# When token chunks enter a wavelet-MLP kernel: two at a time at both ends of the entry, or one per visit throughout

## The chip, the cores and the metric

The kernel runs on one core of one Trainium2 chip. The metric is device microseconds of the whole program. A core has TensorE (PE, matmuls, with PEld for the loading of their stationary operand), VectorE (DVE), ScalarE (ACT), GpSimd (POOL) and SyncE (SP). DMAs are issued from the queues of POOL, SP and ACT and are carried out by the core's 16 DMA engines.

## The reference, cut to what matters

`x` is (8, 4224, 192): batch, tokens, channels. A causal convolution of 7 taps per head runs first, and its result goes into a phase mixer whose large part is a product over all tokens.

```python
# first part: softmax over the 7 taps of each of 8 heads, then
out[b, s, h*24+g] = sum_k w[h, k] * x_pad[b, s + k, h*24+g]      # 6 zero rows ahead
# second part, on x = out
theta = x @ w_theta                       # 192 x 192
zr, zi = x * cos(theta), x * sin(theta)
y = w_tok_r @ zr + w_tok_i @ zi           # 4224 x 4224 over tokens, for each batch
u = x + y
result = u + max(u @ w_ch, 0)
```

## The kernel before

**Tiles.** Batch and channel together are 1536 columns (`N`), in two halves of 768 (`HN`) and four of 384 (`PC`, one PSUM bank in float32). The tokens that are summed over are cut into 33 *chunks* (`NCH`) of 128 tokens. A chunk is four quarters of 32 tokens that lie 33x32 tokens apart (`tokens`). The tokens of the result are cut into 17 *units* (`UNITS`): sixteen pairs of 128-token tiles, and one single tile (unit 16).

**A chunk** is made so. A *window* (class `Window`, L253) is three quarters with the six tokens ahead of each, loaded from `x` by three DMAs on POOL's queue into one of three `xw` tiles (L267). It is convolved by eight matmuls against banded weights (L304) and copied from PSUM into an `xz` tile (L183 on DVE or L185 on ACT). So three chunks take four windows; a chunk's four quarters lie in two or three of them. When a window has been convolved, the next free one is loaded. A chunk (class `Chunk`, L342) is then kept in HBM (`xs`, SP's queue, L355), transposed (L475 on PE for the first eleven chunks, by DMA later), multiplied by `w_theta` (L490), clamped (L378, DVE), and sine and cosine are taken (L406, ACT). The products with x (L415, DVE) and five differences (L427, DVE) leave seven z tiles in one of 11 slots (`SLOTS`).

**A visit** (class `Visit`, L642) is one unit of result rows multiplied with all chunks that are resident in the slots at that time: 14 products of 384 columns for each chunk and visit of a pair (a Strassen-Winograd form of the two-by-two block product), 8 for the single unit (L702, PE). The visit's weights (class `Weights`, L504) are eight DMAs on POOL's queue, four quarters each of `moe_w_tok_r` and `moe_w_tok_i`, cast to bfloat16 into two `st` tiles, one for each matrix (L523). DVE transposes them from there into `w` tiles (L545) and forms four sums or differences (L559). The partial sums of a unit are four `d` tiles in float32. They are loaded from HBM (SP's queue, L664, `d<-part`) when the unit has been visited before, added to from PSUM (L726, twelve times in a visit), and stored again (L741, `part<-d`). Two more evictions of a visit are copies between PSUM banks (L185). In one visit of each unit the convolved x is added to the sums as well (`xr` loads, L671, and additions on POOL, L674). In a unit's last visit the result is finished instead of stored: cast (L836, ACT), transposed, multiplied by `w_ch` (L490), added (L855, DVE) and written out (L862, SP's queue).

**Which chunks are in which visit** is a matter of one tuple, `FIRST`: the visit in which each of the first eleven chunks enters. A chunk stays for 17 visits, so that it has met every unit, and the chunk that takes over its slot enters 17 visits after it:

```python
FIRST = (0, 0, 1, 2, 3, 4, 5, 6, 7, 8, 8)
...
enter = list(FIRST)
for c in range(SLOTS, NCH):
    enter.append(enter[c - SLOTS] + UNITS)
...
for v in range(enter[-1] + UNITS):
    here = [c for c in range(NCH) if enter[c] <= v < enter[c] + UNITS]
    visits.append((ORDER[v % UNITS], here[0], here[-1] + 1))
...
settled = enter[-1]
extra = [v for v in range(len(visits)) if visits[v][2] - visits[v][1] <= SMALL][-EXTRA:]
extra = [v for v in extra if v > settled]
...
    sequence.insert(settled + 2 + 3 * k, v)
```

With it there are 59 visits: 0 to 7 hold 2 to 9 chunks, 8 to 50 hold 11, and 51 to 58 hold 9 down to 2. Chunks enter in visits 0 to 8, 17 to 25 and 34 to 42. The last visits of at most three chunks (`EXTRA` of them at most, here 57 and 58) are taken out of the end and put in between the visits after the last entry: the order there is 42, 43, 58, 44, 45, 57, 46 and so on to 56. `residual_at` (L152) says in which visit a unit gets the convolved x.

**The order of the work.** Each piece above is a `Step` with an engine and an estimated duration. A planner (class `Schedule`, L1005) plays the steps through twice, from due times that come from when the products are wanted, and the second time writes each engine's instructions out in the order that it found. On each engine, and in each issuing queue, the order is then fixed: a step that waits holds up all that stands behind it. The planner picks the PSUM banks of the short matmuls and, for some copies, the engine.

Of the kernel before, what the change touches and what calls it, by code (L numbers as in the profile page):

```python
# [16 lines left out]
def kernel(  # L17
# [39 lines left out]
    NG = 2  # L57
    UNITS = (NT + 1) // 2
    SLOTS = 11
    FIRST = (0, 0, 1, 2, 3, 4, 5, 6, 7, 8, 8)  # L60
    CLAMP = 1.5
    EXTRA = 3
    BY_PE = 4
# [47 lines left out]

    enter = list(FIRST)
    for c in range(SLOTS, NCH):
# [1031 lines left out]
```

## Time and profile before

| | us |
|---|---|
| time, median of 3 runs | 1582.66 |
| lowest and highest run | 1582.4, 1584.01 |
| the profiled execution, its own time | 1582.66 |
| its span, first to last instruction | 1580.9 |

The profile shows one execution. A row of instructions gives engine, operation, output from input, the count, and the mean time of one. A stretch gives for each engine how long it was busy, then the granted TensorE clock as a share of full speed, the DMA share and GB/s. The DMA share is the summed time of packets over that of 16 engines. Packets that overlap each count, so it can pass 1.

The granted clock over the span is 0.956. Four kinds of transfer make up most of the traffic: partial sums (384 KB each, 164 stores, 150 loads of the tile `d` and 14 of the tile `late`, landing after 6.0 to 6.9 us in the median), weights (472 loads, 176 KB each with 11 chunks, 9.8 us), x (132 loads, 114 KB, 14.8 us) and the results (66 stores of 384 KB, 5.0 to 5.5 us).

### The profile page before, as it was taken

Reading aid. Unit: us, or ns where it says so; the run is one execution under the profiler, and the core shown is the slowest. Engines: PE = TensorE matmul, PEld = TensorE weight load, DVE = VectorE, ACT = ScalarE, POOL = GpSimd, SP = SyncE. Lnnn points to the kernel's source line nnn. Section 1 sums busy time; section 2 is a strip of 40 time slices with the busy share of each in tenths; the row PEclk is TensorE's granted clock in tenths of the full one; section 3 lists DMA queues with packets and bytes.
Section 4 is the critical chain, followed back from the end, with each engine's and each line's share of the span. In section 5 each row is a group of like instructions: output and inputs, shape, how many; then the busy total and the mean of one; then the engine's idle time right before and its main releaser. Section 6 shows DMA issues by size and latency. Waiting matters only on the chain.

```text
span 1580.9 us, 24396 instructions
## 1 busy us (share of the span) xinstructions
PE 1434.5 (91%) x9318; PEld 898.2 (57%) x9318; DVE 1076.6 (68%) x1781; ACT 430.7 (27%) x761; POOL 616.7 (39%) x766
## 2 busy tenths in 40 slices
PE   4678899999989989798999996997979999979998
PEld 2345566666655556464666654564646666646665
DVE  5667775435576678566756775865769887666787
ACT  3566461112433124220000321232332212111132
POOL 7645451212543455422312543643534344531220
PEclk6899999999999999898999998998999999999999
DMA  8999998547999999998978999999997999999994
GB/s 60 126 152 167 172 161 153 108 104 134 177 202 225 182 193 216 211 179 170 229 181 178 199 192 166 207 199 196 166 220 179 238 255 236 224 173 196 209 231 151
DMA packets 615269, 289.20 MB, mean 183 GB/s; under 512 B 438800, under 2 KB 565776, under 8 KB 615152
## 3 DMA queue, kind: packets, MB, share of 16 engines
q0 software_dynamic: 451392, 101.19, 61.9%
q1 hardware_dynamic: 123760, 176.62, 40.9%
q10 hardware_dynamic: 40000, 9.84, 4.8%
q8 instruction: 73, 1.20, 0.3%
q14 instruction: 44, 0.36, 0.1%
HBM read 251.60 MB, written 103.42 MB: 225 GB/s over the span
## 4 chain that ended last, share of the span: by engine, by line
PE 50%; DMA 37%; POOL 5%; issue 4%; DVE 3%; SPq 1%; DVEq 0%; ACT 0%; POOLq 0%; ACTq 0%
PE bank L702 46%; DMA xw<-in_x_dram 18%; DMA st<-in_moe_w_tok_i_dram 5%; DMA st<-in_moe_w_tok_r_dram 5%; PE bank L490 3%; DMA xr<-xs 3%; POOL xw L267 2%; DMA uT<-xz 2%; DMA d<-part 1%; DMA part<-d 1%; DMA out_dram<-d 1%; DVE w L545 1%; POOL st L523 1%; POOL d L674 1%; DVE d L726 1%
## 5 line engine op out<-in xcount | busy, mean ns | idle before, releaser
L702 PEld LDWEIGHTS <-w 128*128 128x128 bf16 x7586 | 744.2, 99 | 538.2 <-issue 76.7
L702 PE MATMUL bank<-t,w 128*128 128x384 bf16 x3204 | 567.9, 328 | 11.0 <-DVE d L726 10.1
L545 DVE STREAM_TRANSPOSE w<-st 128x640 bf16<-128x640 bf16 (+4 forms) x412 | 342.9, 856 | 257.1 <-DMA st<-in_moe_w_tok_r_dram 103.2
L702 PE MATMUL bank<-r,w 128*128 128x384 bf16 x2158 | 404.5, 333 | 32.2 <-DVE d L726 16.9
L702 PE MATMUL bank<-i,w 128*128 128x384 bf16 x2224 | 398.8, 330 | 22.1 <-DVE d L726 20.0
L726 DVE TENSOR_TENSOR d<-bank,d 128x384 f32<-128x384 f32 x516 | 275.8, 543 | 155.1 <-PE bank L702 129.9
L523 POOL DMA_DIRECT2D st<-in_moe_w_tok_r_dram x236 | 136.3, 585 | 388.1 <-DVE w L545 333.1
L523 POOL DMA_DIRECT2D st<-in_moe_w_tok_i_dram x236 | 135.4, 579 | 265.5 <-DMA xw<-in_x_dram 128.5
L267 POOL DMA_DIRECT2D xw<-in_x_dram x132 | 189.3, 1440 | 98.9 <-PE bank L304 45.5
L559 DVE TENSOR_TENSOR w<-w 128x1408 bf16<-128x1408 bf16 (+8 forms) x216 | 182.4, 844 | 2.3
L185 ACT ACTIVATE xz<-bank 32x384 bf16<-32x384 f32 (+2 forms) x299 | 139.9, 482 | 147.6 <-issue 84.0
L674 POOL TENSOR_TENSOR d<-d,xr 128x768 f32<-128x768 f32 x60 | 100.6, 1678 | 115.8 <-DMA xr<-xs 58.3
L185 ACT ACTIVATE bank<-bank 128x384 f32<-128x384 f32 x109 | 51.1, 474 | 240.3 <-PE bank L702 232.2
L406 ACT ACTIVATE r<-ang,half_pi 128x768 bf16<-128x768 f32 x44 | 41.0, 932 | 276.0 <-DVE ang L378 275.8
L185 ACT ACTIVATE d<-bank 128x384 f32<-128x384 f32 x127 | 60.8, 490 | 159.9 <-PE bank L702 159.4
L490 PE MATMUL bank<-wth,uT 128*128 128x192 bf16 x528 | 67.4, 269 | 34.6 <-DVE ang L378 20.2
L378 DVE TENSOR_SCALAR ang<-bank 128x384 f32<-128x384 f32 x132 | 70.0, 549 | 34.8 <-PE bank L490 33.9
L490 PEld LDWEIGHTS <-uT 128*128 128x128 bf16 x632 | 60.4, 106 | 56.6 <-issue 27.3
L304 PE MATMUL bank<-xw,bands 114*128 114x192 bf16 x352 | 54.3, 255 | 27.8 <-DMA xw<-in_x_dram 8.5
L836 ACT ACTIVATE ubT<-d 128x768 bf16<-128x768 f32 x42 | 35.4, 842 | 160.3 <-DVE d L726 146.5
L304 PEld LDWEIGHTS <-bands 114*128 114x128 bf16 x352 | 34.7, 101 | 47.7 <-issue 21.1
L855 DVE SCALAR_TENSOR_TENSOR d<-bank,d 128x384 f32<-128x384 f32 x104 | 53.8, 547 | 10.8 <-PE bank L490 9.8
(76 smaller groups left out, 563.8 us busy)
## 6 DMA issues: line engine op xcount, KB each, us to landing
part<-d SPq DMA_DIRECT2D x164, 384.0 KB, 6.7
d<-part SPq DMA_DIRECT2D x150, 384.0 KB, 6.9
st<-in_moe_w_tok_r_dram POOLq DMA_DIRECT2D x160, 176.0 KB, 9.8
st<-in_moe_w_tok_i_dram POOLq DMA_DIRECT2D x160, 176.0 KB, 9.8
out_dram<-d SPq DMA_DIRECT2D x52, 384.0 KB, 5.5
xw<-in_x_dram POOLq DMA_DIRECT2D x131, 114.0 KB, 14.8
xs<-xz SPq DMA_DIRECT2D x132, 96.0 KB, 8.4
xr<-xs POOLq DMA_DIRECT2D x66, 192.0 KB, 8.4
```

What stands on the lines that cost most here:

```text
L185: act(nc.scalar.activation(out=o(), in_=i(*b), func=AT.Copy))
L267: pool(nc.gpsimd.dma_start(out=xw[self.k][lo : lo + n, :, :], in_=x[:, t0 : t0 + n, :].rearrange("b s d -> s b d"),))
L304: pe(nc.tensor.matmul(banks[b][:, hh * B * G : (hh + 1) * B * G], lhsT=bands[:, h, at : at + NQ, :].rearrange("p z m -> p (z m)"), rhs=xw[ ...
L378: "dve", 0.55, lambda b, k2=k2, g=g: dve(nc.vector.tensor_scalar(out=self.ang[g][:, k2 * 2 * D : (k2 + 1) * 2 * D], in0=banks[b][:, 0 : 2 ...
L490: pe(nc.tensor.matmul(banks[bk][:, b * D : (b + 1) * D], lhsT=tT[:, 3 * k + b + i, :], rhs=w[:, 2 * b + i, :], start=(i == 0), stop=(i == ...
L523: "pool", 0.58, lambda a=a, t0=t0, i=i, w=w: pool(nc.gpsimd.dma_start(out=st[i][a * Q : (a + 1) * Q, 0:nb, 0 : n * Q], in_=w[r0 : r0 + nb ...
L545: lambda c=c, ce=ce: dve(nc.vector.transpose(self.tile(name)[:, c:ce, :, :], st[i][:, at : at + NQ, c * Q : ce * Q].rearrange("p bt (c j) ...
L559: s = Step("dve", 0.15 + 0.069 * n, lambda: dve(nc.vector.tensor_tensor(out=flat(self.tile(name)), in0=flat(self.tile(p)), in1=flat(self.t ...
L674: a = Step("pool", 1.75, lambda: pool(nc.gpsimd.tensor_tensor(out=tile_(), in0=tile_(), in1=xrt[k], op=ALU.add)), [r, s])
L702: pe(nc.tensor.matmul(banks[bank][:, 0:PC], lhsT=self.w.block(a, c), rhs=chunks[c].operand(b, g), start=(start and c == self.lo), stop=(c ...
L726: dve(nc.vector.tensor_tensor(out=o, in0=y, in1=o, op=ALU.add))
L855: dve(nc.vector.scalar_tensor_tensor(out=dk, in0=banks[b][:, 0:PC], scalar=0.0, in1=dk, op0=ALU.max, op1=ALU.add,))
```

## The change

One line: the first chunk enters in visit 0, the next in visit 1, and so on to chunk 10 in visit 10.

```diff
@@ -57,7 +57,7 @@
     NG = 2
     UNITS = (NT + 1) // 2
     SLOTS = 11
-    FIRST = (0, 0, 1, 2, 3, 4, 5, 6, 7, 8, 8)
+    FIRST = (0, 1, 2, 3, 4, 5, 6, 7, 8, 9, 10)
     CLAMP = 1.5
     EXTRA = 3
     BY_PE = 4
```

What follows from it in the lists: 61 visits; 0 to 9 hold 1 to 10 chunks, 10 to 50 hold 11, and 51 to 60 hold 10 down to 1. Chunks enter one in a visit, in visits 0 to 10, 17 to 27 and 34 to 44. The visits that are put in between the others are 60, 59 and 58, and the order at the end is 44, 45, 60, 46, 47, 59, 48, 49, 58, 50, 51 and so on to 57. The planner plays the steps through anew, so the order on every engine can differ everywhere.

## The prediction

> **What bounds the kernel now.** I read the head of the page first.
>
> ```profile
> span 1580.9 us, 24396 instructions
> PE 1434.5 (91%) x9318; PEld 898.2 (57%) x9318; DVE 1076.6 (68%) x1781; ACT 430.7 (27%) x761; POOL 616.7 (39%) x766
> ...
> PE   4678899999989989798999996997979999979998
> ...
> DMA  8999998547999999998978999999997999999994
> ```
>
> PE is the bound, with 146 us of idle in 1580.9. The DMA digits fall below 9 where PE stays at 9 (slices 7 to 10, 21 and 22). So the idle has to be looked for by stage. I counted the products of line 702 in order of time (14 per chunk and visit, 8 for unit 16) to find where each visit starts, and asked for the busy table of those stretches. Neighbouring visits interleave a little, so the limits are good to about 1 us.
>
> ```profile
> 54.60:79.20 24.60, 14.48 (x84) 8.54 (x84) 13.49 (x29) 12.83 (x26) 13.10 (x14) 0.81 1.14 144
> 218.70:246.30 27.60, 27.60 (x189) 17.65 (x188) 23.55 (x40) 12.63 (x22) 10.66 (x15) 1.00 1.35 162
> 411.10:443.40 32.30, 29.39 (x205) 18.88 (x203) 20.89 (x30) 15.07 (x28) 17.01 (x15) 1.00 1.34 197
> 530.60:570.90 40.30, 30.83 (x180) 18.86 (x179) 23.70 (x38) 7.61 (x14) 20.82 (x24) 0.87 1.29 207
> 570.90:597.90 27.00, 27.00 (x180) 17.03 (x179) 22.86 (x38) 8.05 (x14) 14.52 (x16) 1.00 1.28 192
> 729.50:754.50 25.00, 25.00 (x155) 15.05 (x154) 15.83 (x25) 0.95 (x2) 4.55 (x8) 1.00 0.87 199
> 1219.30:1282.40 63.10, 62.70 (x434) 40.80 (x432) 55.78 (x95) 12.50 (x18) 29.32 (x40) 1.00 1.12 238
> ```
>
> After the stretch come its length, then busy time of PE, PEld, DVE, ACT and POOL, granted clock, DMA share and GB/s. The rows are visits 1, 8, 16, 20, 21, 26, and 43+58+44. A full visit (11 chunks) in which no chunk enters takes 25.0 us at DMA share 0.87; one in which a chunk is prepared takes 27.0 us when it goes well, so a chunk's convolution and mix cost PE 2.0 us. While chunks enter, the DMA share is about 1.3, and some visits are far longer.
>
> The second entry (visits 16 to 25) took 32.3, 29.9, 29.1, 28.2, 40.3, 27.0, 27.7, 39.4, 29.4 and 35.1 us: 318.4, where 10x25.0 + 11x2.0 = 272 are needed, so 46 us are lost. The third (33 to 42) took 32.7, 27.7, 45.8, 27.0, 29.8, 42.1, 27.0, 29.6, 37.9 and 25.0: 324.6, 53 lost. The waits, over the whole span, tell what the lost time is (us in total, times, longest):
>
> ```profile
> PE bank L702 <- DVE d L726: 47.1, 16, 11.5
> ...
> PE bank L490 <- DVE ang L378: 20.2, 7, 6.7
> ...
> DVE w L545 <- DMA st<-in_moe_w_tok_r_dram: 103.2, 14, 19.2
> ...
> POOL st L523 <- DMA xw<-in_x_dram: 175.3, 65, 6.5
> ```
>
> Read upwards: POOL's queue holds weight loads back until x loads have landed; the weights come late; DVE stands in order at the transpose; the evictions queued behind it (L726, L378) come late, and PE has no bank. The long visits are 20, 23, 25 and 35, 38, 41. Windows hold three quarters and a chunk four, so every third chunk (12, 15, 18, 21, 24, 27, 30) needs two windows, and each convolved window releases three x loads. The long visits are those that take in chunks 15, 18, 21 and 24, 27, 30. They are bursts, tied to chunks.
>
> **The change part by part.** The chunk-visits stay 561, so products, conversions, x loads and mixes stay the same in number. From the lists of lines 112 to 128: 61 visits in place of 59; sizes 1 to 10 at the start, eleven from visit 10 to 50, then 10 down to 1. In all, two visits of 11 become two of 10 and two of 1. Chunks enter one per visit at 0 to 10, 17 to 27 and 34 to 44. The lists of residual visits come out the same, so 43 and 44, which have one, now lie inside the third entry.
>
> Two visits add: 16 weight loads (POOL, 585 ns each by the L523 rows: 9.4 us), eight loads and eight stores of 384 KB on SP's queue (units 11 and 7 get a fourth visit; their last visits, 59 and 60, go between 45 and 50), and 24 evictions of 543 ns (13.0 us of DVE). None of it is PE work. All of it lies beside PE unless a queue is late, so I price it by stage.
>
> *Start.* Visit k now needs chunk k, where visit k-1 needed it. So new visit k answers to old visit k-1, with one chunk-visit more done (14 matmuls, about 2.3 us) and one weight set more loaded: that of one chunk. POOL pays 8x0.58 = 4.6 us for it in the queue in which the x loads stand, and its loads must land: the nearest rows are those of two chunks (32.0 KB), 2.8 and 6.0 us median. 4.6 + 4 (between these) - 2.3 = +6, less what idle POOL hides (13.1 busy of 24.6 in visit 1): **+4**. Lower end -2 (all hidden, one chunk-visit gained); upper end: the second rival below. Chunk 10's later date gains nothing: visit 8, which takes chunks 9 and 10, already runs without PE idle.
>
> [...] No run here has shown a set of one chunk.
>
> *Second entry.* What goes is the double entry: visit 16 at 32.3 us against 25.0 + 2x2.0 = 29, and visit 25, which took two chunks and three windows. From the first 3 us come back; of the second's 8 over 27.0 only 1, since chunk 21 still has its burst. Against that chunk 12's burst moves from the relaxed visit 16 to visit 17, where loads are already dense: +2. Sum **-2**; ends -17 (two visits' worth of relief, first rival) and +4 (third rival).
>
> *Third entry.* Double entry gone: 32.7 against 29, -3. Residual visits 43 and 44 now meet x loads: four residual loads and four adds each, 4x(0.6+1.65) = 9 us of POOL per visit in front of weight loads; visit 42 had 25.0 us with no wait at all. A burst stall is 11 to 19 us here (37.9 to 45.8 less 27.0); I take less than half of one, +5. Sum **+2**; ends -17 and +26.
>
> The clock is a part of each stall: visit 20 lost 13.3 us, of which its waits are 9.4 (6.3 on L378 and 3.1 on L726); the rest goes with its clock of 0.87. The prices above are whole visit times and hold this already. [...]
>
> *Final part.* Visit 60 (one chunk) has its fixed work: 12 evictions x 0.543 = 6.5, eight output additions (L855, 0.547) = 4.4, small transposes and sums 3 (bounded by the rows of two chunks, 0.44 and 0.29 each): 14 us of DVE where PE works 14x0.161 + 32x0.08 = 5 (25.0 us for 154 products, and half of that for the 32 narrower output matmuls). The excess of 9 meets the slack of its neighbours: 63.1 - 55.8 = 7 in the last row of the table, for three visits. So 2 stay, and 2 more for the 16 transfers of 384 KB beside DMA share 1.12: **+4**. Ends 0 and +9.
>
> Sum: +4 - 2 + 2 + 4 = +8. The profiled execution took 1582.66 us, span 1580.9 and 1.8 around it, and is the median itself. 1582.66 + 8 = 1590.7.
>
> **The rivals.** *Relief (faster).* If the entries are bound by DMA throughput and not by bursts, spreading wins. Clean stretches move about 0.84 of a share (47.5% + 36.3% of the two big queues, 720 to 880 us) in 25 us, 21 units a visit; entries run at 1.30. A visit more in an entry then costs 21/1.30 = 16 us there and takes 25 us out of the clean stretch: -9 per entry for one visit, -17 for two. For it: every entry visit stands at 1.28 to 1.35. Against it: visits 21 and 22 run at 27.0 and 27.7 at that same share. It decides if a burst's stall shrinks below about 8 us. 4 + 4 - 9 - 9 = -10: 1572.7.
>
> *Start paced by weight sets.* Old visits 0 to 8 start at 27.3, 54.6, 79.2, 104.7, 123.4, 145.7, 171.8, 194.5 and 218.7 us, and sets are issued some 21 us apart, whatever their size. If each new visit still takes its old slot, visit 10 starts with 55 chunk-visits done instead of 66: 11x2.27 = 25 us instead of 4: 1612. Against it: the first set is small and visit 0 waits for no second chunk.
>
> *The dense rate holds throughout.* Visits 18 to 24 average 31.6 us and 35 to 41 average 34.2, with one chunk each. Eleven such visits and a clean one are 372.6 and 401 us, against 368.4 and 375 for the same twelve visits now: +4 and +26. With 4 and 4: 1620.7. Against it: three windows are loaded before each entry, and the third entry's last chunks release no loads.
>
> *No net effect.* Terms of single microseconds cancel; 1582.7.
>
> **How the numbers follow.** A measurement of this kernel tells about 0.2% (3.2 us) from no change. Forecast 0.38, relief 0.32, set-paced start 0.10, dense rate 0.08, no net effect 0.12. So faster 0.32, within 0.2% 0.12, slower 0.56. The forecast's own range, from its terms, is 1586 to 1604. To hold 8 in 10, it goes down to 1566, taking in relief but for its far end, and up to 1616, with the set-paced start and without the dense rate.
>
> **What would show it.** L523 with 488 issues, part<-d with 172. Visit 10 starting near 250 us with 55 chunk-visits done (start +4); near 271, the set-paced rival. Long visits at 21, 24, 27 and 36, 39, 42, each 35 us or more, and visit 16 near 27: bursts. If these fall under 33 us, relief was right. Visit 60's neighbours over 29 us would confirm the final term. I am wrong if PE's idle falls below 140 us.

## The result, and the profile after

| | before | after |
|---|---|---|
| median of four runs, us | 1583.34 | 1596.04 |
| lowest and highest | 1582.4, 1584.57 | 1591.87, 1616.18 |
| profiled execution, its span | 1580.9 | 1595.0 |

The changed kernel is slower, by under 1%: ratio 1.0071, 95% interval 1.0049 to 1.0093. The forecast was 1590.7 us, slower. A second comparison, told below, gave 1.0121 (1.0066 to 1.0177). Ratios here and below leave out single runs more than 1.5% above the fastest of their kernel: 1616.18 here, and seven of the ten runs of the pair-at-end kernel below.

The head of the page after:

```profile
span 1595.0 us, 24505 instructions
...
PE 1442.9 (90%) x9318; PEld 900.5 (56%) x9318; DVE 1085.3 (68%) x1823; ACT 429.5 (27%) x763; POOL 623.6 (39%) x782
...
PE   4668998999979969799899997798989999899998
...
DMA  8999998467999999999879999999999999999994
```

PE has the same 9318 matmuls. It idles 152 us (1595.0 - 1442.9) where it idled 146, and the other 8 us of the 14 stand as busy time (1442.9 against 1434.5), with the mean granted clock at 0.953 in place of 0.956. DVE's count grew by 42, POOL's by 16, the added weight loads. Visits can be found as before, by counting the products of line 702. The rows below are visits 1, 9, 16, 18, 21, 22, 24, 48 and 45+60+46; the columns are those shown of before (length, busy PE, PEld, DVE, ACT, POOL, clock, DMA share, GB/s):

```profile
45.90:68.40 22.50, 12.34 (x71) 6.64 (x72) 13.51 (x30) 11.19 (x20) 13.70 (x16) 0.75 1.13 140
223.00:255.30 32.30, 27.24 (x178) 17.22 (x176) 19.50 (x32) 12.54 (x23) 10.83 (x15) 0.95 1.12 148
394.70:422.60 27.90, 27.21 (x180) 16.96 (x178) 16.63 (x26) 12.09 (x22) 12.01 (x13) 1.00 1.17 149
452.70:489.30 36.60, 29.97 (x181) 18.16 (x179) 23.68 (x41) 7.61 (x14) 11.21 (x15) 0.91 1.33 203
544.10:588.50 44.40, 31.49 (x180) 18.93 (x178) 25.09 (x38) 7.61 (x14) 21.33 (x24) 0.85 1.27 181
588.50:615.50 27.00, 27.00 (x180) 17.05 (x178) 22.10 (x38) 8.05 (x14) 18.16 (x20) 1.00 1.10 222
643.60:684.70 41.10, 30.55 (x180) 18.75 (x178) 23.64 (x42) 7.61 (x14) 11.45 (x16) 0.88 1.30 199
1342.50:1379.80 37.30, 31.20 (x205) 19.71 (x203) 25.19 (x42) 5.71 (x8) 14.12 (x20) 0.95 1.21 228
1256.40:1321.70 65.30, 63.51 (x429) 40.58 (x427) 50.85 (x93) 12.78 (x18) 24.73 (x35) 0.97 0.99 210
```

The bursts are there, each one visit later: chunks 12, 15 and 18 enter in visits 18, 21 and 24, which take 36.6, 44.4 and 41.1 us. The two windows of such a chunk are convolved in the visit before; the long visit is the next one, where the late weights are missed. Visit 22, after such a burst, takes the full-speed 27.0. The doubled visit 16 is gone (27.9 in place of 32.3). New are visit 9 at 32.3 us and visit 48 at 37.3.

The waits of the whole span, after, with the chain that the prediction read (us in total, times, longest):

```profile
PE bank L702 <- DVE d L726: 40.2, 15, 10.0
PE bank L490 <- DVE ang L378: 35.2, 10, 6.7
...
PE bank L702 <- DVE w L545: 20.4, 5, 9.7
...
DVE w L545 <- DMA st<-in_moe_w_tok_r_dram: 115.0, 20, 16.0
...
POOL st L523 <- DMA xw<-in_x_dram: 193.1, 75, 8.0
```

POOL's queue holds weight loads back behind x loads for 193 us instead of 175, and DVE waits longer for weights.

To compare times at equal work, I take the moments when 66, 264 and 429 chunk-visits are done. Before, these are the starts of visits 10, 28 and 43; after, of 11, 29 and 44. Each kernel has two traces, the second from the runs told below. All in us:

| stretch | before, two traces | after, two traces | difference of the means | forecast |
|---|---|---|---|---|
| start, to 66 | 271.4, 267.7 | 280.3, 278.3 | +9.7 | +4 |
| second entry, to 264 | 508.1, 515.5 | 515.6, 523.7 | +7.9 | -2 |
| third entry, to 429 | 439.8, 437.6 | 435.5, 430.1 | -5.9 | +2 |
| final part, to the end | 361.6, 353.9 | 363.6, 366.7 | +7.4 | +4 |

Two executions of one kernel differ by up to 8 us in a stretch, so of these differences only that of the start stands well clear of the scatter. The first traces alone give +8.9, +7.5, -4.3 and +2.0, which is the 14.1 us between the spans.

### The profile page after: what moved, and what is told of

The parts are those of the page before. It is cut to its first block, busy times and chain, and to the rows that moved or that the text cites. A ratio compares the mean times of both kernels' runs of the same rounds, so it can differ in the third digit from the quotient of the medians.

```text
span 1595.0 us, 24505 instructions
## 1 busy us (share of the span) xinstructions
PE 1442.9 (90%) x9318; PEld 900.5 (56%) x9318; DVE 1085.3 (68%) x1823; ACT 429.5 (27%) x763; POOL 623.6 (39%) x782
## 3 DMA queue, kind: packets, MB, share of 16 engines
q0 software_dynamic: 455744, 101.19, 60.6%
## 4 chain that ended last, share of the span: by engine, by line
DMA 29%; PE 27%; issue 7%; POOL 6%; DVE 4%; SPq 1%; ACTq 0%; ACT 0%; DVEq 0%; POOLq 0%
PE bank L702 24%; DMA st<-in_moe_w_tok_r_dram 10%; DMA st<-in_moe_w_tok_i_dram 7%; DMA xw<-in_x_dram 6%; POOL xw L267 3%; PE bank L490 2%; POOL d L674 2%; DVE w L545 2%; DMA ubT<-ubT 2%; DVE d L726 1%; DMA uT<-ub 1%; DMA part<-d 1%; POOL st L523 1%; DMA d<-part 1%; DMA out_dram<-late 1%
## 5 line engine op out<-in xcount | busy, mean ns | idle before, releaser
L545 DVE STREAM_TRANSPOSE w<-st 128x640 bf16<-128x640 bf16 (+5 forms) x416 | 342.1, 847 | 278.5 <-DMA st<-in_moe_w_tok_r_dram 115.0
L702 PE MATMUL bank<-r,w 128*128 128x384 bf16 x2154 | 408.7, 334 | 28.7 <-DVE w L545 19.6
L726 DVE TENSOR_TENSOR d<-bank,d 128x384 f32<-128x384 f32 x542 | 286.8, 542 | 133.2 <-PE bank L702 108.2
L523 POOL DMA_DIRECT2D st<-in_moe_w_tok_i_dram x244 | 140.0, 579 | 349.8 <-DMA xw<-in_x_dram 156.7
L523 POOL DMA_DIRECT2D st<-in_moe_w_tok_r_dram x244 | 140.8, 584 | 325.3 <-DVE w L545 273.8
L559 DVE TENSOR_TENSOR w<-w 128x1408 bf16<-128x1408 bf16 (+10 forms) x220 | 182.9, 831 | 2.4
L185 ACT ACTIVATE xz<-bank 64x384 bf16<-64x384 f32 (+2 forms) x300 | 139.9, 481 | 144.9 <-issue 75.2
L378 DVE TENSOR_SCALAR ang<-bank 128x384 f32<-128x384 f32 x132 | 70.2, 551 | 30.8 <-PE bank L490 30.2
L304 PEld LDWEIGHTS <-bands 114*128 114x128 bf16 x352 | 34.7, 102 | 41.0 <-issue 15.6
## 6 DMA issues: line engine op xcount, KB each, us to landing
st<-in_moe_w_tok_r_dram POOLq DMA_DIRECT2D x152, 176.0 KB, 10.4
xw<-in_x_dram POOLq DMA_DIRECT2D x131, 114.0 KB, 13.7
```

The source lines that it names most:

```text
L185: act(nc.scalar.activation(out=o(), in_=i(*b), func=AT.Copy))
L304: pe(nc.tensor.matmul(banks[b][:, hh * B * G : (hh + 1) * B * G], lhsT=bands[:, h, at : at + NQ, :].rearrange("p z m -> p (z m)"), rhs=xw[ ...
L378: "dve", 0.55, lambda b, k2=k2, g=g: dve(nc.vector.tensor_scalar(out=self.ang[g][:, k2 * 2 * D : (k2 + 1) * 2 * D], in0=banks[b][:, 0 : 2 ...
L523: "pool", 0.58, lambda a=a, t0=t0, i=i, w=w: pool(nc.gpsimd.dma_start(out=st[i][a * Q : (a + 1) * Q, 0:nb, 0 : n * Q], in_=w[r0 : r0 + nb ...
L545: lambda c=c, ce=ce: dve(nc.vector.transpose(self.tile(name)[:, c:ce, :, :], st[i][:, at : at + NQ, c * Q : ce * Q].rearrange("p bt (c j) ...
L559: s = Step("dve", 0.15 + 0.069 * n, lambda: dve(nc.vector.tensor_tensor(out=flat(self.tile(name)), in0=flat(self.tile(p)), in1=flat(self.t ...
```

## The experiments

Theory Q: weight loads wait in POOL's queue behind x loads, in bursts of two windows for every third chunk, and DVE and PE wait for the weights. Its rivals were that the start is paced by weight sets (T), that DMA throughput binds the entries (R), and that the difference is an accident of the written order (P).

**Half of the change each.** Only the pair at the end of an entry taken apart, and only the pair at its start:

```diff
-    FIRST = (0, 0, 1, 2, 3, 4, 5, 6, 7, 8, 8)
+    FIRST = (0, 0, 1, 2, 3, 4, 5, 6, 7, 8, 9)      # pair left at the start
...
+    FIRST = (0, 1, 2, 3, 4, 5, 6, 7, 8, 9, 9)      # pair left at the end
```

> The first half of the change undone: chunks 0 and 1 enter together in visit 0, as before the change, and only the pair at the end of an entry (chunks 9 and 10) is taken apart; 60 visits. Theory Q (the weight sets wait in POOL's queue behind x loads; the start pays for the added set of one chunk, and the entries pay for a burst of two windows at every third chunk): no one-chunk set is loaded at the start, so the start's +9 us of the changed kernel is gone and about 0 to +4 is left, near 1585 us. Rival T (the pace of the start is one weight set per visit, whatever its size): visit 9 alone comes a slot later, +3 to +5 by itself, about 1588. Rival P (the difference of 13 us is an accident of the order that the planner writes): any time between 1575 and 1600, with long visits in other places than at chunks 15, 18, 21.

> The second half undone: chunk 0 enters alone in visit 0, chunks 9 and 10 together in visit 9; 60 visits. Theory Q: the start pays for the added set, +9 us when 66 chunk-visits are done, the rest as before, about 1592. Rival T: the same sign, larger, since every visit from 0 to 9 stands one chunk behind: up to +25. Rival P: 1575 to 1600 with no clear stage.

Measured: with the pair left at the start 1594.63 us, ratio 1.0108 (1.0045 to 1.0171); with the pair left at the end 1587.65, ratio 0.9938 (0.9875 to 1.0002), and 1.0015 by the medians of all runs. The totals went against theory Q's numbers: the kernel without the one-chunk set was the slower one, and the other is not told from no change. In these comparisons single times of the kernel before reach from 1573 to 1603 us, so a half of 13 us is at their limit. The traces are clearer on the start. The pair-at-start kernel begins visit 10 at 273.3 us with 65 chunk-visits done; one more at 2.27 us gives 275.6 for 66, +4.2 against 271.4. The pair-at-end kernel begins visit 11 at 279.4 with 67, so 277.1, +5.7. Together that is 9.9, where the whole change showed 8.9 in the first pair of traces. So the added set costs about what was forecast, and taking chunks 9 and 10 apart, which I had priced at nothing, costs nearly as much. Each half has one trace, though, and the start of the kernel before differed by 3.7 us between its two (271.4 and 267.7): both halves show a cost, but their sizes are rough. The long visits mostly go with the chunks, as theory Q has it: 17, 20, 23, 35 and 38 with the pair left at the start (40.7, 35.7, 40.3, 45.6 and 42.7 us; 18, with 36.2, does not fit), 21, 24 and 36 with the pair left at the end (37.9, 43.6 and 44.9).

**The x loads cut into 32 and 6 rows**, in both kernels, with the written order of all other steps kept:

```diff
 def load(lo=lo, t0=t0, n=n):
-    pool(nc.gpsimd.dma_start(
-        out=xw[self.k][lo : lo + n, :, :],
-        in_=x[:, t0 : t0 + n, :].rearrange("b s d -> s b d"),
-    ))
+    for r, m in ((0, Q), (Q, n - Q)):
+        if m:
+            pool(nc.gpsimd.dma_start(
+                out=xw[self.k][lo + r : lo + r + m, :, :],
+                in_=x[:, t0 + r : t0 + r + m, :].rearrange("b s d -> s b d"),
+            ))
```

> The kernel before with each x load of 38 rows issued as two DMAs, of 32 and of 6 rows. The same bytes and the same order of steps; the planner is not told. In the trace of before, the one x load of 32 rows took 710 ns to issue and landed in 3.0 us, five of 38 rows near it took 1440 ns and landed in 9.4, with thousands of packets of 4 bytes beside them. Theory Q: x loads land in under 6 us in place of 14.8, POOL's waits on them (175 us) fall under 60, most of the long visits at chunks 15, 18, 21, 24, 27 and 30 come down to 27 to 29 us, and the start shortens: 1490 to 1540 us. Rival R (the entries are bound by the bytes and rows that the DMA engines move, and spreading would relieve them): the rows are the same, so the entries stay at DMA share 1.3 and 46 and 53 us of loss: 1570 to 1590.

> The changed kernel with the same split of the x loads. Theory Q: its start no longer pays 9 us for one more set, since the set no longer waits behind x loads; it stands within 6 us of the split kernel before, on either side. Rival T: the weight sets still pace the start and it stays 9 us or more behind. Rival P: the difference of 13 us stays or changes sign without a stage to show for it.

Measured: 1430.58 us from the kernel before, ratio 0.9057 (0.9001 to 0.9113), and 1446.81 from the changed one, 0.9156 (0.9101 to 0.9212). The gain was larger than theory Q expected, and rival R's 1570 to 1590 us are out. The page of the split kernel before (line numbers move by two):

```profile
PE 1400.7 (98%) x9318; PEld 885.2 (62%) x9318; DVE 1080.9 (76%) x1781; ACT 430.6 (30%) x761; POOL 578.9 (40%) x897
```

Its waits on POOL (us in total, times, longest):

```profile
POOL st L525 <- DMA xw<-in_x_dram: 7.6, 8, 2.1
```

Its DMA issues of x (KB each, median us to landing):

```profile
xw<-in_x_dram POOLq DMA_DIRECT2D x132, 96.0 KB, 4.5
...
xw<-in_x_dram POOLq DMA_DIRECT2D x131, 18.0 KB, 4.7
```

POOL's wait for x loads is 7.6 us where it was 175, a load lands in 4.5 where it took 14.8, and no visit of the entries takes over 29.0 us. The bursts came from the slow x loads. How they hold the weights can be read from visit 20 of the kernel before. POOL issues six x loads and two weight loads, and then waits (start and length in us):

```profile
510.19 1.49 POOL L267 DMA_DIRECT2D xw<-in_x_dram  x1 [2.30 <-PE bank L304]
513.09 7.17 POOL L267 DMA_DIRECT2D xw<-in_x_dram  x5 [1.41 <-DMA st<-in_moe_w_tok_r_dram]
520.23 1.20 POOL L523 DMA_DIRECT2D st<-in_moe_w_tok_r_dram  x2
527.00 0.58 POOL L523 DMA_DIRECT2D st<-in_moe_w_tok_r_dram  x1 [5.57 <-DMA xw<-in_x_dram]
532.19 0.58 POOL L523 DMA_DIRECT2D st<-in_moe_w_tok_r_dram  x1 [4.61 <-DMA xw<-in_x_dram]
```

DVE then stands at the transpose until the fourth has landed:

```profile
549.17 0.98 DVE L545 STREAM_TRANSPOSE w<-st 128x768 bf16<-128x768 bf16 x1 [11.78 <-DMA st<-in_moe_w_tok_r_dram]
```

By the issue and landing times in the trace, the six x loads land one after another from 526.7 to 542.4 us and the four weight loads behind them from 545.1 to 549.1. So the weights are held twice. Before their issue: the program's DMAs on POOL's queue signal on eight semaphores in turn (102 to 109 in the trace), and each of the 65 waits that make up the 175 us was for the DMA eight places ahead to land. And after it: none of the 678 DMAs of this queue landed before one that was issued ahead of it. Both hold in all twelve traces. A second way is not set apart: the split also takes small packets off the DMA engines (23424 of 4 bytes on this queue in place of 289616), and stores of partial sums, which go by SP's queue, land in 4.7 us where they took 6.7.

With the x loads split, the two kernels stand level up to the final part: 220.8 against 222.2 us at 66 chunk-visits, then 464.0 against 464.3, and 388.6 against 389.2. So what the change costs in the start and the entries it costs only through slow x loads. What is left is the final part, 356.6 against 364.3. The totals, 16 us apart by the medians and 10 by the profiled executions, do not stand within the 6 us that theory Q had asked for.

**Both kernels again, unaltered.**

> The changed kernel once more, unaltered, against the kernel before. It is to tell how much of the 13 us is the kernel and how much the scatter of executions, which in the last comparison reached from 1573 to 1603 us for the kernel before. Theory Q: slower again, by 4 to 16 us; the long visits stand in the same places (18, 21, 24 and 36, 39, 42), each with a length of its own that moves by several us between executions. Rival P: no difference that holds, -5 to +5 us, and the long visits elsewhere.

> The kernel before once more, unaltered, for a second trace. Theory Q: long visits again at 20, 23, 25 and 35, 38, 41, none in the clean stretches; each stage's time within 10 us of the first trace's (271 us to visit 10, 508 to visit 28, 440 to visit 43, 362 to the end). Rival P: long visits elsewhere, since what is late is a matter of chance.

Measured: the changed kernel 1600.88 us (1590.52 to 1608.96), ratio 1.0121 (1.0066 to 1.0177); the kernel before, one execution, 1576.5. The ratio is above the expected 4 to 16 us at its middle (1600.88 - 1578.7 = 22), but slower again. Long visits stand in nearly the same places: 18, 21, 24 at 35.3, 41.8 and 47.1, and 36, 39, 42 at 43.2, 41.1 and 34.2 in the changed kernel; 20, 23, 24 at 37.8, 40.3 and 41.2, and 35, 38, 41 at 44.7, 43.5 and 38.7 in the other, where visit 17 now had 37.5 too and 25, long in the first trace and named by theory Q, took 25.0. Each moves by some us between executions (visit 23 after: 28.1, then 34.7). The chunk of a burst is fixed, its visit to within one, its size is not. An accident of order without a place is out.

**Fewer visits, on split x loads.** `FIRST = (0, 0, 0, 1, 2, 3, 4, 5, 6, 6, 6)`, otherwise as the split kernel before.

> The change's opposite, on the kernel before with split x loads: chunks 0 to 2 enter together in visit 0 and 8 to 10 in visit 6, so 57 visits in place of 59, with x loads that no longer hold the weights up. Theory V (once the queue is clear, what is left of the change is the fixed work of two more visits, about 8 us each by the two split kernels: 1430.6 and 1446.8): 1410 to 1422 us. Rival B (chunks that enter three at a time starve the visit that takes them; spreading was right in itself): 1430 to 1450, with visits 6, 17 and 23 of 35 us or more.

Measured: 1480.29 us, 50 more than the split kernel before. Theory V's forecast fell. Its price of 8 us a visit was not tested alone, since entering three at a time came with it. The rival was right in kind, but its 1430 to 1450 us were 30 too low. Against the split kernel before, the start is 9.5 us longer, the entries 24.7 and 16.0, and the final part 1.7 shorter. Visits 6, 17, 23 and 34, each of which takes in three chunks, are long (the fifth, 40, is not, at 25.7 us). Their stretches, with the columns as above:

```profile
143.90:180.30 36.40, 32.45 (x218) 20.67 (x216) 28.58 (x49) 20.80 (x36) 11.37 (x20) 0.95 0.80 145
424.00:461.40 37.40, 33.69 (x212) 21.09 (x211) 29.26 (x52) 15.76 (x27) 12.16 (x20) 0.91 0.94 182
604.80:643.90 39.10, 33.20 (x195) 20.02 (x194) 30.05 (x48) 13.15 (x24) 16.72 (x28) 0.87 1.06 193
887.50:928.00 40.50, 33.97 (x203) 20.81 (x202) 32.03 (x51) 14.99 (x27) 22.97 (x33) 0.87 0.96 176
```

The DMA share is low here, at most 1.06 where undisturbed entry visits stand at 1.10 to 1.35. PE stands in short waits on the preparation of chunks (ACT's copies into `xz`, DVE's products), 3.7 to 6.4 us in a visit, which is about all of its idle time there; the lower clock, 0.87 to 0.95, goes with the rest. Over the whole span two of them stand as (us in total, times, longest):

```profile
PE bank L306 <- ACT xz L185: 10.8, 15, 1.4
...
PE bank L704 <- DVE t L429: 3.6, 6, 1.3
```

So entering three at a time costs, and with the x loads split one or two at a time does not. That ACT and DVE set the price is read from these waits; no run tests it. Spreading is right up to a point; the kernel before had already reached it.

**The small last visits further apart**, on split x loads:

```diff
-        sequence.insert(settled + 2 + 3 * k, v)
+        sequence.insert(settled + 2 + 4 * k, v)
```

> The changed kernel with split x loads, and with the three small last visits put in four places apart in place of three (after visits 45, 48 and 51). In the changed kernel, split or not, visit 48 took 37 to 38 us and PE waited 4 to 5 us there for a transposed output, right behind the small visit 59. Theory V: the three small visits bring their outputs too close together; further apart, the part from visit 44 to the end falls from 364 us to 357 to 360, and the time to about 1440. Rival: the fixed work of one more visit costs this wherever it lies, and the time stays at 1445 to 1449.

> The kernel before with x loads of 32 and 6 rows, and its two small last visits put in four places apart in place of three. It is the partner of the changed kernel with the same two edits (1436.5 us). Theory V (outputs of small visits too close together cost the changed kernel its final part; with two small visits there is little to crowd): 1425 to 1432, and the gap to the changed kernel 4 to 11 us instead of 16. Rival: the spacing helps any kernel by the same 10 us: 1418 to 1422.

Measured: the changed kernel 1436.45 us, 10 less than the 1446.81 with spacing three, though these come from different comparisons; its visit 48 takes 28.3 us where it took 37.8, and the wait on `uT<-ub` is not in its list. The kernel before 1430.0, as with spacing three (1430.58). So by the medians the gap between the two falls from 16 to 6 us. By the profiled executions it falls only from 10.0 to 8.4, and in the final part from 7.7 (364.3 against 356.6) to 5.0 (360.6 against 355.6; 357 to 360 were expected): visits 52 to 54, now behind the small visit 58, take 72.2 us in place of 62.9. The crowding of the small visits costs something, and spacing moves it; how large a part of the final part's cost it is stays open. In the split kernel with spacing three the wait itself is this (visit 48, us in total, times, longest):

```profile
PE bank L492 <- DMA uT<-ub: 4.9, 1, 4.9
```

**What made the x loads slow.** Two halves of 19 rows in place of 32 and 6:

> The kernel before with each x load of 38 rows issued as two DMAs of 19 rows each, in place of 32 and 6. It tells apart two readings of the split's gain. Theory D (what costs is the packets of 4 bytes that go with a load: 289616 of them in the kernel before, 23424 with 32 and 6 rows): 19 rows bring as many small packets as 38 or more, and the time stays at 1560 us or above, long visits included. Rival S (smaller loads are enough, since weights can slip in between): 1430 to 1490 us, as with 32 and 6.

Measured: 1820.61 us, ratio 1.1545 (1.142 to 1.1671): slower even than one load of 38 rows. The software queue's rows (packets, MB, share of 16 engines) of the kernel before, the split one and the halved one:

```profile
q0 software_dynamic: 451392, 101.19, 61.9%
```

```profile
q0 software_dynamic: 185200, 100.12, 53.1%
```

```profile
q0 software_dynamic: 772080, 102.47, 69.9%
```

The halved kernel's DMA issues of x:

```profile
xw<-in_x_dram POOLq DMA_DIRECT2D x262, 57.0 KB, 14.3
```

The megabytes agree within 2.5%; the packets do not. Counted by size, 289616, 23424 and 610304 of them are of 4 bytes, while those of 384 and 704 bytes are the same in number. Half a load lands as long after its issue as a whole one (14.3 against 14.8 us). Most of that time is waiting behind the loads ahead. What a load adds to a busy queue is the time from the landing before it to its own: 3.4 us in the median for 38 rows, 2.7 for 19, and 0.9 and 0.3 for 32 and 6. Among these four shapes the added time does not go with the size (2.7 us for the 57 KB of 19 rows, 0.9 for the 96 KB of 32): smaller loads are not enough. Why loads of 38 and of 19 rows come with so many packets of 4 bytes, and loads of 32 and 6 with few, no run shows.

## Why the prediction was right or wrong

**Direction and the mechanism of the lost time: right.** The burst at every third chunk was named from the long visits of before, and with it the places after. Of the six named, 21, 24, 36, 39 and 42 came with 35 us or more in both traces (34.2 once); 27 did not (29.4 and 26.8). Visit 16 came down to 27.9, 488 weight loads and 172 stores were there, and PE's idle is over 140 us. The split of the x loads shows the cause of the bursts: without the slow loads, every one of these visits of the changed kernel runs at 25 to 28 us. But the bursts are not what made the change slower. The two entries together moved by 2 us, within the scatter; the start and the final part carry the difference, and the final part does so with fast x loads too.

**The relief rival: wrong, for the reason given.** The two entries together came out 2 us longer in the mean, where relief asked for 18 less, and the bursts kept 34 to 47 us. Spreading did not shrink a burst; a shorter landing did (4.5 us in place of 14.8 in the kernel before), at nearly the same bytes (100.12 MB in place of 101.19). The dense-rate rival asked for +4 and +26 us in the two entries; the third came at -5.9.

**Start, +4 forecast, +9.7 measured.** The step that failed is "chunk 10's later date gains nothing", read as no cost either. The added set was sized well as far as one trace can tell (+5.7 in its own, nearer to the +6 that the prediction had before it took off what idle POOL hides; the loads of one chunk, 16 KB each, landed in 3.7 and 2.3 us in the changed kernel). But visit 9 took 32.3 us where 22.7 + 2.0 for a chunk were due (25.4 with the x loads split). PE waits there on a copy of DVE (us in total, times, longest):

```profile
PE bank L490 <- DVE uT L183: 5.1, 1, 5.1
```

DVE makes that copy behind transposes of late weights:

```profile
240.90 3.29 DVE L545 STREAM_TRANSPOSE w<-st 128x768 bf16<-128x768 bf16 x4 [9.48 <-DMA st<-in_moe_w_tok_i_dram]
244.12 0.52 DVE L183 COPY uT<-bank 128x768 bf16<-128x768 bf16 x1
```

One more weight set, of nearly full size, now stands in the queue before chunk 10 is done. The pair-at-start kernel shows +4.2 for this alone, with 34.7 us in its visit 8. The set-paced rival is out: visit 10 began at 255.3 us with 55 chunk-visits done, near the 250 of the forecast and not near 271.

**Second entry, -2 forecast, +7.9 measured.** The step that failed is that the bursts of chunks 15 and 18 would stay as they were, a term put at nothing. What each burst lost, in us over the same visits of the split kernel:

| burst of chunk | before, two traces | after, two traces |
|---|---|---|
| 12, with the doubled visit of before | 8.3, 16.0 | 12.9, 10.2 |
| 15 | 13.7, 10.7 | 17.4, 14.8 |
| 18 | 11.8, 12.6 | 14.5, 27.1 |
| 21 | 10.4, 12.2 | 6.5, 7.4 |

In the means chunk 12 comes out level (forecast -1), chunk 21 gives back some 4 us (forecast 1), and chunks 15 and 18 cost 3.9 and 8.6 more. With 12.6 us between two executions at one burst, two traces cannot say how much of this is the change; why these two bursts were larger stays open.

**Third entry, +2 forecast, -5.9 measured.** The step that failed is the +5 for the residual visits 43 and 44: they took 27.6 and 25.0 us, where 27.0 and 25.0 are needed. The last x load is issued at 1160.7 us, before visit 43 begins at 1203.8, so there was nothing left for the residual loads to collide with; the prediction had said this itself against another rival. The -3 for the doubled visit was right or low (32.7 and 30.8 before, 27.0 after). This miss lies within the ends that were given (-17 and +26); that of the second entry lies above its upper end of +4.

**Final part, +4 forecast, +7.4 measured.** The form was wrong. Of visit 60's neighbours, 27.7 and 31.6 us, only one came over the 29 that would have confirmed the term, and those of the small visits of before took 28.3 to 29.6 as well. The longest visit is 48, which the prediction did not name: 37.3 and 40.9 us, with PE waiting for a transposed output (4.4 us in the first trace) right behind the small visit 59. The part's length goes with the number of small visits in it: 351.3 to 361.6 us in the six traces with two, 360.6 to 366.7 in the five with three, but 354.9 in the one with one. That the outputs crowd each other is shown for visit 48 alone; the plain fixed work of one more visit is not ruled out for the rest. The first pair of traces shows only +2.0 in this part, since before had a stall in visit 49 there (38.9 us, 32.0 in the second trace).

The sum of +8 against 12.7 was near by luck, because the misses had both signs. It was no better than its terms.

## What to carry to other kernels

When a schedule is spread over more visits, price what each added visit puts into the shared queue ahead of the thing that is waited for; here spreading the same loads left the bursts at 34 to 47 us, since what hurt was how long one load blocks the queue (3.4 us each, in the median). Look at the landing time of each transfer beside one of nearly the same shape: the 96 KB load that landed in 3.0 us beside 114 KB ones at 9.4 (14.8 over the whole run) was worth some 150 us, more than ten times the change studied. And when one part is moved late, ask what already stands there: small work units put close together showed a wait that was gone when they stood further apart, though most of the time was not.

## What the runs showed of the hardware that was not expected

A casting load of 38 rows on POOL's queue costs about 2000 more packets of 4 bytes than the same rows as 32 and 6 ((289616 - 23424) / 131), takes 1440 ns to issue instead of 583 for each part, and adds 3.4 us to a busy queue instead of 0.9 and 0.3. Halves of 19 rows, at 2.7 us each, are worse still. The DMAs of POOL's queue landed strictly in the order of their issue in all twelve traces, so a slow load delays all that are issued behind it. That one edit takes the kernel from 1585 to 1431 us. With the small visits three or four places apart it stays at 1430, and this is the fastest version that was run.
